# A gated linear scan with a soft mixture of experts on one core: slot sums divided behind the experts, some gates by sigmoid, PSUM banks held in pairs, and a new order table

## The chip, the cores and the metric

The kernel runs on one core of one Trainium2 chip. The metric is the device time of one execution in microseconds (us). The core has five instruction streams that work side by side: PE (the matrix engine; "PEld" is its weight load), DVE (vector), ACT (scalar, table functions), POOL (a second vector engine) and SP, which here only issues DMAs. SBUF holds tiles of 128 partitions; PSUM has 8 banks of 128 x 512 float32, which PE writes and DVE and ACT read.

## The reference, cut to what matters

```python
# x, r_gate, i_gate: (4, 5056, 256); 20224 tokens of 256 channels
log_a = 8.0 * sigmoid(r_gate) * log(sigmoid(a_param))      # per token and channel
a_t = exp(log_a)
x_gated = sqrt(max(1 - a_t * a_t, 1e-6)) * sigmoid(i_gate) * x
h = a_t[:, t] * h + x_gated[:, t]                           # along the 5056 tokens of a batch: y
logits = y @ phi                                            # 32 slots, 8 experts of 4
d = exp(logits - logits.max(0));  d /= d.sum(0) + 1e-9      # over all 20224 tokens
slot_input = d.T @ y                                        # (32, 256)
slot_out[e] = relu(slot_input[e] @ w1[e]) @ w2[e]           # w1 (8,256,1024), w2 (8,1024,256)
c = exp(logits - logits.max(1));  c /= c.sum(1) + 1e-9
out = c @ slot_out
```

## The kernel before, in words

Line numbers of before stand first, those after the change behind a slash.

**Windows.** The tokens are cut into 40 windows of 512 (the last has 256), and the windows into units of one or two. For each window three DMAs bring r, i and x. PE transposes r into PSUM (`rp`, L383/L394), so that channels lie on partitions and time lies along a row, and ACT reads each half of that from its bank into `A` (`sr`, L393/L406: tanh of r/2). Per unit ACT takes the sigmoid of i (`si`, L405/L427), POOL multiplies i by x (`u`, L412/L434), ACT forms a_t (`ex`, L425/L448 and L450, an Exp whose scale and bias are read from a 128 x 1 column), POOL squares it (`sq`, L433/L458) and ACT takes the square root of 1 - a² (`qr`, L440/L465). PE transposes u into PSUM (`up`, L450/L475); DVE multiplies it there, in place, by the root (`st`, L460/L485) and scans along time (`sc`, L473/L498), reading the bank. PE transposes the scanned rows back (`yp`, L493/L518), and DVE or ACT copies them out of PSUM (`yc`, L281 and L279/L288 and L286). Every such step is named by window and half: `sc 22 1` is the scan of window 22, half 1.

**Groups.** Four windows make a group: logits (`lp`, L539/L573), their running maximum on DVE (`ls`, L549 and L552/L583 and L586), the factor for the older groups on ACT (`md`, L557/L591), transposes of the logits (`ep`, L563/L597), their Exp on ACT (`ee`, L572/L606), the weighted sums on PE (`acc`, L581/L615) and their accumulation on DVE (`as`, L592/L626).

**Slots and experts.** Behind the last group some small steps form the weights of the groups (`Wt`). In before `sp` (L656 and L657) sums the groups with them, tokens' sums and denominators both, and `slot` (L662 to L664) takes the reciprocal of the denominators and multiplies. The experts run in four pairs (`hp` L713/L755, `hs`, `ht`, `hr`, `so` L740/L782), then `s0`, `s1` and `s2` spread their result.

**Tokens.** For each group the weights c over the slots are formed (`ct`, `c0`, `cm`, `c1` L802/L847, `c2`, `c3`, `hc`, `hx`), PE multiplies (`op`, L839/L884: 16 matmuls into four banks), DVE and ACT copy the four banks out (`og`, L281 and L279/L288 and L286) and a DMA of 512 KB stores each window.

**What sets the order.** Every step is an operation with a number; the string `ORDER` lists the numbers, `b` behind one puts it on its second engine. `Plan.order` walks the list with costs written in the code, starts an operation when its engine, its inputs and its buffers are free, and so chooses the buffers; the instructions are then emitted in that order, each engine takes its own in that order, and the framework puts in the waits between engines, which keep the accesses to each tile in the order of the program. ACT holds one table of functions at a time; the list groups the square roots of three or four units, then the sigmoids, then the exponentials, with a table load at each change.

Of the kernel before, what the change touches and what calls it, by code (L numbers as in the profile page):

```python
# [8 lines left out]
F32 = mybir.dt.float32  # L9
# [8 lines left out]
N_ES = 2  # L18
TABLE_US = 1.283
# [22 lines left out]
394 434 454 475 495 862 417 395 320 863 360 864 865 361 866 396 418 397 338 297 340 398 399 339b 435 321 322b  # L42
341b 298b 414 415 379 868 380b 476 400 416 381 362 299 363 419 300 489 629 507 529 651 508 432 632 382 453 472
436 439 875 613 633 614 513 473 876 656 437 440 877 634 455 458 869 878 515 867 635 597 657 438 441 480 459 481
456 879 460 457 494 514 870 871 872 873 477 401 420 654 442 556 880 516 536 874 478 482 402 421 403 422 423b 655
496 499 404 443 497 500 444 461 445 479 462 498 517 598 618 557 577 881 518 882 521 463 883 884 886 501 522 519
464 523 502 503 520 589 711 530 733 611 549 671 571 548 570 885 535 483 714 485 887 504 540 524 630 590 612 652
752 693 774 599 558 554 555 595 576 617 888 541 526 486b 715 738 739 675 736 525b 636 737 527 542 505 537 538
757 559 755 697 673 756 758 484 539 674 676 677 562 560 563 543 578 716 717 889 698 561 579 564 544 581 779 695
890 777 696 780 778 891 580 638 720 679 582 631 653 793 672 694 596 603 604 637 658 622 619 600 641 892 893 894  # L50
895 620 583 601 623 605 602 678 897 898 624 639 659 721 741 680 700 640 899 621 584 585 586 565 587b 566b 567
660 642 896 625 626b 568b 545 643 546 661 606 722 607b 681 663 627 644 628 645 662 646 608 796 901 682 685 713
815 963 754 753 975 712 776 794 795 734 983 775 816 817 735 699 902 900 761 609b 718 908 701 686 664 683 665 702
# [33 lines left out]
class Plan:  # L87
# [42 lines left out]
    def order(self):  # L130
        out = []
# [775 lines left out]
```

## Time and profile before

| | us |
|---|---|
| median of 3 runs | 307.64 (307.35 to 307.68) |
| the profiled execution | 307.92 |
| its span, first to last instruction | 306.1 |
| PE, DVE, ACT, POOL busy | 241.1, 238.0, 246.1, 181.7 |
| mean granted TensorE clock | 0.928 |

The profile is of one execution. A row "L393 ACT ACTIVATE g<-b ... x78 | 41.5, 609 | 2.5 <-PE b L383" reads: line 393, on ACT, from a bank (b) into a buffer (g), 78 instructions, 41.5 us in all, 609 ns the mean of one, and 2.5 us in which ACT stood idle ahead of them, mostly until the PE instruction of line 383 had ended. A row of the stretches lists for each engine the busy time inside the stretch and the number of instructions, then the granted clock of PE (1.00 is full speed), the mean busy share of the DMA engines and their GB/s.

### The profile page before, as it was taken

What the parts mean: (1) busy time and instruction counts of PE and PEld (TensorE: products, weight loads), DVE (VectorE), ACT (ScalarE), POOL (GpSimd) and SP (SyncE); (2) the same over time, 40 slices, a digit from 0 to 9 for tenths busy, and PEclk for the clock granted to TensorE, in tenths of its full rate; (3) what the DMA queues carried; (4) which work ended last, traced back from release to release, by engine and by line L of the source; (5) the groups of instructions that cost most, each with busy time, mean ns of one, the idle gap of its engine ahead of it and who ended that gap; (6) DMA issues with size and microseconds to landing.
All of it is one profiled execution on the core that took longest, in us unless ns stands there. A gap on an engine that the chain in (4) does not pass through costs nothing.

```text
span 306.1 us, 5779 instructions
## 1 busy us (share of the span) xinstructions
PE 241.1 (79%) x2134; PEld 170.0 (56%) x2134; DVE 238.0 (78%) x370; ACT 246.1 (80%) x311; POOL 181.7 (59%) x121
## 2 busy tenths in 40 slices
PE   3605797969888896988989788878999999898900
PEld 3604665737646754766577464736563677656700
DVE  0003999699999998999999989979967869975600
ACT  5999999999999999999999999997220457874320
POOL 1389986988598899699599996991000241031000
PEclk9955999999999999799999999999999999995565
DMA  7999999967998993998856997999990019999996
GB/s 252 415 405 408 408 376 412 396 255 286 399 383 323 410 365 122 378 413 281 327 207 238 384 363 305 335 385 349 406 359 6 2 60 401 405 403 407 361 409 269
DMA packets 28032, 100.03 MB, mean 327 GB/s; under 512 B 3362, under 2 KB 3364, under 8 KB 28004
## 3 DMA queue, kind: packets, MB, share of 16 engines
q1 hardware_dynamic: 28004, 99.66, 84.8%
q8 instruction: 17, 0.28, 0.4%
q14 instruction: 11, 0.09, 0.1%
HBM read 78.94 MB, written 20.71 MB: 326 GB/s over the span
## 4 chain that ended last, share of the span: by engine, by line
PE 25%; ACT 25%; DVE 15%; issue 9%; POOL 6%; DMA 3%; ACTq 0%; SPq 0%; DVEq 0%; POOLq 0%
PE b L839 7%; ACT g L425 7%; DVE g L473 6%; ACT g L393 5%; DVE b L460 4%; ACT g L405 4%; POOL g L412 3%; ACT g L440 3%; POOL g L433 2%; DVE y L281 2%; PE b L713 2%; PE b L740 2%; PE b L493 2%; PE b L450 2%; ACT y L279 2%
## 5 line engine op out<-in xcount | busy, mean ns | idle before, releaser
L412 POOL TENSOR_TENSOR g<-g,g 128x1024 f32<-128x1024 f32 (+1 forms) x40 | 92.7, 2347 | 10.6 <-ACT g L405 10.1
L433 POOL TENSOR_TENSOR g<-g 128x1024 f32<-128x1024 f32 (+1 forms) x40 | 73.8, 1873 | 25.0 <-ACT g L425 21.9
L460 DVE SCALAR_TENSOR_TENSOR b<-g,b 128x512 f32<-128x512 f32 (+1 forms) x80 | 51.5, 677 | 31.4 <-ACT g L440 30.2
L450 PE MATMUL b<-ident,g 128*128 128x128 f32 x316 | 47.6, 286 | 21.7 <-POOL g L412 15.5
L493 PE MATMUL b<-ident,g 128*128 128x128 f32 x316 | 46.9, 283 | 10.4 <-DVE g L473 4.1
L450 PEld LDWEIGHTS b<-ident,g 128*128 128x128 f32 x316 | 35.8, 145 | 34.1 <-POOL g L412 17.7
L383 PE MATMUL b<-ident,g 128*128 128x128 f32 x316 | 46.5, 288 | 8.1 <-DMA g<-in_r_gate_dram 3.2
L473 DVE TENSOR_TENSOR_SCAN g<-g,g,b 128x512 f32<-128x512 f32 x40 | 50.3, 1271 | 0.2
L473 DVE TENSOR_TENSOR_SCAN g<-g,b 128x512 f32<-128x512 f32 (+7 forms) x46 | 49.2, 1094 | 0.3
L493 PEld LDWEIGHTS b<-ident,g 128*128 128x128 f32 x316 | 35.1, 143 | 23.7 <-DVE g L473 8.6
L425 ACT ACTIVATE g<-g,ca 128x1024 f32<-128x1024 f32 (+2 forms) x44 | 47.5, 1158 | 0.0
L810 POOL TENSOR_TENSOR y<-y,rs 128x512 f32<-128x512 f32 x10 | 10.4, 1048 | 61.3 <-DVE rs L807 59.8
L383 PEld LDWEIGHTS b<-ident,g 128*128 128x128 f32 x316 | 36.4, 146 | 18.0 <-ACT g L393 4.3
L393 ACT ACTIVATE g<-b 128x512 f32<-128x512 f32 x80 | 42.2, 605 | 2.5 <-PE b L383 2.4
L281 DVE COPY y<-b 128x512 f32<-128x512 f32 x55 | 36.4, 678 | 6.9 <-PE b L814 3.5
L405 ACT ACTIVATE g<-g 128x2048 f32<-128x2048 f32 (+2 forms) x22 | 38.2, 1755 | 0.1
L440 ACT ACTIVATE g<-g 128x2048 f32<-128x2048 f32 (+2 forms) x22 | 37.2, 1736 | 0.1
L279 ACT COPY g<-b 128x512 f32<-128x512 f32 x47 | 24.7, 593 | 14.3 <-PE b L839 13.5
L839 PE MATMUL b<-soR,y 32*128 32x256 f32 x320 | 31.2, 462 | 3.4 <-DVE y L281 2.3
L839 PEld LDWEIGHTS b<-soR,y 32*128 32x128 f32 x320 | 22.0, 219 | 10.0 <-ACT g L279 3.2
L281 DVE COPY g<-b 128x512 f32<-128x512 f32 x33 | 21.0, 680 | 5.1 <-PE b L839 4.8
L279 ACT COPY y<-b 128x512 f32<-128x512 f32 x34 | 18.7, 592 | 5.9 <-PE b L493 5.9
(83 smaller groups left out, 244.0 us busy)
## 6 DMA issues: line engine op xcount, KB each, us to landing
g<-in_x_dram SPq DMA_DIRECT2D x39, 512.0 KB, 6.7
g<-in_i_gate_dram SPq DMA_DIRECT2D x39, 512.0 KB, 8.1
out_dram<-g SPq DMA_DIRECT2D x39, 512.0 KB, 6.2
g<-in_r_gate_dram SPq DMA_DIRECT2D x38, 512.0 KB, 6.6
g<-in_moe_w_dram SPq DMA_DIRECT2D x32, 512.0 KB, 6.3
g<-in_r_gate_dram SPq DMA_DIRECT2D x3, 256.0 KB, 5.8
g<-in_i_gate_dram SPq DMA_DIRECT2D x1, 256.0 KB, 8.9
g<-in_x_dram SPq DMA_DIRECT2D x1, 256.0 KB, 8.8
```

Source lines behind the costliest of these rows:

```text
L281: nc.vector.tensor_copy(out=dst, in_=srct)
L383: nc.tensor.transpose(out=by_tile(rp, n)[:, j, :], in_=rows(("r", w), n)[:, j, h * P : (h + 1) * P], identity=ident,)
L393: nc.scalar.activation(halves(("A", w))[:, h, :c], Bk(("rp", w, h))[:, :c], AF.Tanh, scale=0.5)
L405: nc.scalar.activation(a, a, AF.Sigmoid)
L412: nc.gpsimd.tensor_tensor(out=rows(("x", w), n), in0=rows(("i", w), n), in1=rows(("x", w), n), op=ALU.mult)
L425: nc.scalar.activation(a, a, AF.Exp, scale=ca[:, h : h + 1], bias=ca[:, h : h + 1])
L433: nc.gpsimd.tensor_tensor(out=halves(("N", w))[:, :, :c], in0=a, in1=a, op=ALU.mult)
L450: nc.tensor.transpose(out=by_tile(up, n)[:, j, :], in_=rows(("x", w), n)[:, j, h * P : (h + 1) * P], identity=ident,)
L460: nc.vector.scalar_tensor_tensor(up, halves(("N", w))[:, h, :c], 1e-3, up, op0=ALU.max, op1=ALU.mult)
L473: nc.vector.tensor_tensor_scan(dst, dst, up[:, s0:s1], init, op0=ALU.mult, op1=ALU.add)
L493: nc.tensor.transpose(out=yp[:, j, h * P : (h + 1) * P], in_=halves(("A", w))[:, h, (2 * i + j) * P : (2 * i + j + 1) * P], identity=ident,)
L839: nc.tensor.matmul(Bk(("op", w0, n))[:, i * D : (i + 1) * D], hT()[r, (2 * i2 + i) * P : (2 * i2 + i + 1) * P], soR[r, :], start=True, sto ...
```

## The change

- The third pair of `sp` matmuls, which summed the denominators, and the two DVE steps that divided are gone; `slot` is one copy. In their place `dn` (four small matmuls, L698) and `rd` (an addition and a reciprocal on 128 x 1, L703 and L704) run later, and `s2`, behind the experts, multiplies by `rd`.
- Where all `sr` of a unit are emitted while the sigmoid table is loaded, `sr` takes Sigmoid instead of tanh, and `ex` reads only a scale column (`ca8`, eight times the logarithm) and no bias column. This holds for 6 units: 12 of the 44 `ex` instructions (L448).
- The 8 PSUM tiles of one bank (`bank`) become 4 tiles of two banks (`banks`, 128 x 2 x 512), and `Bk` returns a half of one. Variants that would use both halves at once are written but are switched off (`WIDE_R`, `WIDE_Y`).
- The planner's costs are written anew, `acc` also depends on the first `yc` of each window, and `ORDER` is a new list of 1237 operations (1235 before). There are 24 table loads in both. ACT does 25 of the `yc` copies instead of 29.

```diff
+WIDE_R = False
+WIDE_Y = False
...
 ORDER = """
-1 74 96 5 33 11 115 55 13 12 34 56 75 116 4 35 219 137 57 241 97 159 301 76 138 160 98 179 201 117 2 0 6 7 8 9
+1 74 96 5 115 2 0 3 6 7 8 9 10 77 79 101 99 118 78 102 80 100 119 120 83 121 11 16 14 15 33 55 36 58 124 17 60
...
-    bank = [ps.tile([P, C], F32, name=f"b{i}") for i in range(8)]
+    banks = [ps.tile([P, 2, C], F32, name=f"b{i}") for i in range(4)]
...
     def Bk(key):
-        return bank[plan.place[key]]
+        i = plan.place[key]
+        return banks[i // 2][:, i % 2, :]
...
     def e_decay3(o):
+        nc.vector.tensor_scalar(ca8, ca, 8.0, None, op0=ALU.mult)
         nc.vector.tensor_scalar(ca, ca, 4.0, None, op0=ALU.mult)
...
+    def plain(unit):
+        return all(plan.by_key[("sr", v, h)].table == "S" for v in unit for h in range(1 if WIDE_R else H))
...
-                nc.scalar.activation(halves(("A", w))[:, h, :c], Bk(("rp", w, h))[:, :c], AF.Tanh, scale=0.5)
+
+                f, k = (AF.Sigmoid, 1.0) if plain(unit) else (AF.Tanh, 0.5)
+                nc.scalar.activation(halves(("A", w))[:, h, :c], Bk(("rp", w, h))[:, :c], f, scale=k)
...
-                    nc.scalar.activation(a, a, AF.Exp, scale=ca[:, h : h + 1], bias=ca[:, h : h + 1])
+                    if plain(unit):
+                        nc.scalar.activation(a, a, AF.Exp, scale=ca8[:, h : h + 1])
+                    else:
+                        nc.scalar.activation(a, a, AF.Exp, scale=ca[:, h : h + 1], bias=ca[:, h : h + 1])
...
-               deps=[("ee", t), ("acc", t, j - 1)] + [("yc", w, j // 2) for w in ws],
+               deps=[("ee", t), ("acc", t, j - 1)] + [("yc", w, i) for w in ws for i in {0, j // 2}],
...
     def e_sp(o):
         for h in range(H):
             nc.tensor.matmul(sp()[:, h, :], accS[:, h * P : (h + 1) * P], Wt, start=True, stop=True)
-        nc.tensor.matmul(
-            sp()[:, H, :], accS[:, D : D + 1].broadcast_to([P, P]), Wt, start=True, stop=True
-        )
...
     def e_slot(o):
-        nc.vector.tensor_scalar(rd, sp()[:, H : H + 1, :], 1e-9, None, op0=ALU.add)
+        nc.vector.tensor_copy(out=slotT, in_=sp())
+
+
+    def e_dn(o):
+        for j in range(J):
+            nc.tensor.matmul(
+                Bk(("dn",))[32 * j : 32 * j + NS, :1], Wt, accS[:, D : D + 1], start=True, stop=True
+            )
+
+    def e_rd(o):
+        nc.vector.tensor_scalar(rd, Bk(("dn",))[:, :1], 1e-9, None, op0=ALU.add)
         nc.vector.reciprocal(rd, rd)
-        nc.vector.tensor_tensor(out=slotT, in0=sp()[:, :H, :], in1=rd.broadcast_to([P, H, NS]), op=ALU.mult)
...
     def e_s2(o):
-        copy(o, soR, Bk(("sr",))[:, :D])
+        if o.on == "ACT":
+            nc.scalar.activation(soR, Bk(("sr",))[:, :D], AF.Copy, scale=rd)
+        else:
+            nc.vector.tensor_scalar(soR, Bk(("sr",))[:, :D], rd, None, op0=ALU.mult)
```

The rows below stand as the built programs have them: line, operation, target<-source with the number of each tile, shape, and the engines (and DMA rings) whose semaphores the instruction waits on. A tile b is PSUM: in before b0_88 to b7_95 are one bank each, after the change b0_88 to b3_91 are two banks each, and the two halves bear one name.

**ACT behind the roots of windows 6 to 11.** In before ACT ends the sigmoids of this phase with these rows; the last four are `sr 20 1`, `sr 18 0`, the table load and the first exponential of windows 12 and 13:

```order
L393 ACTIVATE g6_67<-b2_90 128x512 [waits PE_49]
L393 ACTIVATE g6_67<-b1_89 128x512 [waits DVE_49,PE_49]
L393 ACTIVATE g13_74<-b3_91 128x512 [waits PE_49,Pool_49]
L405 ACTIVATE g1_62<-g1_62 128x2048 [waits DMAHW2_49,DMAHW1_49,Activation_49]
L393 ACTIVATE g13_74<-b6_94 128x512 [waits DVE_49,PE_49]
L393 ACTIVATE g2_63<-b4_92 128x512
L425 ACT_TABLE_LOAD
L425 ACTIVATE g16_77<-g16_77,ca_108 128x2x512
```

After the change ACT has there the last sigmoids of this phase, with `sr 14 1` and `sr 27 0` (the third and fourth row), the exponential of windows 12 and 13, and behind it `sr 16 0`, which reads a half of b3 and waits for DVE:

```order
L406 ACTIVATE g18_79<-b0_88 128x512 [waits PE_49]
L427 ACTIVATE g10_71<-g10_71 128x2048 [waits DMAHW5_49,DMAHW2_49]
L406 ACTIVATE g1_62<-b1_89 128x512 [waits PE_49]
L406 ACTIVATE g18_79<-b2_90 128x512
L450 ACT_TABLE_LOAD
L450 ACTIVATE g3_64<-g3_64,ca_104 128x2x512 [waits Activation_49]
L450 ACTIVATE g3_64<-g3_64,ca_104 128x2x512
L406 ACTIVATE g16_77<-b3_91 128x512 [waits DVE_49,PE_49]
L406 ACTIVATE g16_77<-b0_88 128x512 [waits PE_49]
```

What moved: eleven `sr` instead of eight stand between the roots and this table load, and the semaphore that `sr 16 0` waits on at DVE stands for `yc 7 1`, the copy out of the other half of b3.

**DVE at windows 7 to 10.** In before the two multiplications of window 9 (the third and fourth row) come behind `ls 1`, and a copy and the scans of the same window follow:

```order
L549 TENSOR_SCALAR l1_97,m1_121<-b0_88,m0_120 128x512 [waits PE_49]
L552 SCALAR_TENSOR_TENSOR n1_132<-b0_88,m1_121,minus_110 128x1 [waits DVE_49]
L460 SCALAR_TENSOR_TENSOR b5_93<-g10_71,b5_93 128x512 [waits DMAHW3_49,Pool_49]
L460 SCALAR_TENSOR_TENSOR b1_89<-g10_71,b1_89 128x512 [waits PE_49,Activation_49]
L281 COPY y1_81<-b7_95 128x2x256
L473 SCALAR_TENSOR_TENSOR g0_61<-g0_61,b5_93 128x448 [waits DVE_49]
L473 SCALAR_TENSOR_TENSOR g0_61<-g0_61,b5_93 128x64
L473 SCALAR_TENSOR_TENSOR g0_61<-g0_61,b1_89 128x448 [waits DVE_49]
```

After the change window 9, half 1 (`st 9 1`, the fourth row) comes first of windows 8 and 9, straight behind the last scan of window 7:

```order
L485 SCALAR_TENSOR_TENSOR b2_90<-g18_79,b2_90 128x512 [waits DVE_49]
L288 COPY y0_80<-b1_89 128x2x256 [waits PE_49]
L498 SCALAR_TENSOR_TENSOR g16_77<-g16_77,b2_90 128x512 [waits PE_49,Activation_49]
L485 SCALAR_TENSOR_TENSOR b2_90<-g8_69,b2_90 128x512 [waits PE_49,DMAHW7_49,Activation_49,Pool_49]
L485 SCALAR_TENSOR_TENSOR b3_91<-g8_69,b3_91 128x512
L485 SCALAR_TENSOR_TENSOR b3_91<-g8_69,b3_91 128x512 [waits DVE_49]
L498 SCALAR_TENSOR_TENSOR g11_72<-g11_72,g16_77,b3_91 128x512 [waits DVE_49]
```

What moved: `st 9 1` works in a half of b2, and the ACT semaphore that it waits on stands for `sr 27 0`, which reads the other half of b2 (the fourth row of the ACT piece above). Behind it on DVE stand windows 8 to 10 and, sixteen rows on, `yc 7 1`.

**ACT and DVE behind the roots of windows 18 to 23.** In before ACT had, from the last of these roots on:

```order
L440 ACTIVATE g12_73<-g12_73 128x2048 [waits Pool_49]
L405 ACT_TABLE_LOAD [waits DMAHW4_49]
L405 ACTIVATE g7_68<-g7_68 128x2048 [waits DMAHW2_49]
L393 ACTIVATE g15_76<-b3_91 128x512 [waits DMAHW6_49,DVE_49,PE_49]
L393 ACTIVATE g0_61<-b4_92 128x512 [waits DVE_49,PE_49]
L405 ACTIVATE g1_62<-g1_62 128x2048 [waits DMAHW5_49,DMAHW4_49]
L572 ACT_TABLE_LOAD
L572 ACTIVATE e0_86<-b0_88 128x512 [waits Activation_49]
```

After the change it has, from the first copy behind these roots on, `ee 3` and `sr 31 0` as the last two rows:

```order
L286 COPY y3_83<-b2_90 128x2x256 [waits DVE_49]
L427 ACT_TABLE_LOAD [waits DMAHW7_49]
L427 ACTIVATE g12_73<-g12_73 128x2048 [waits DMAHW4_49]
L406 ACTIVATE g13_74<-b0_88 128x512 [waits PE_49,Activation_49]
L406 ACTIVATE g13_74<-b0_88 128x512
L406 ACTIVATE g15_76<-b1_89 128x512 [waits DVE_49,PE_49]
L427 ACTIVATE g2_63<-g2_63 128x2048 [waits DMAHW1_49,DMAHW0_49]
L406 ACTIVATE g11_72<-b3_91 128x512 [waits DVE_49,PE_49,Pool_49]
L591 ACT_TABLE_LOAD
L591 ACTIVATE d3_142<-m2_119,n3_131 128x1
L606 ACTIVATE e0_86<-b1_89 128x512 [waits DVE_49,PE_49]
L406 ACTIVATE g13_74<-b2_90 128x512 [waits DVE_49,PE_49]
```

And on DVE, after the change, the end of window 21, the first half of window 22, `ls 4` (its two rows in the middle) and `sc 22 1` behind it:

```order
L498 SCALAR_TENSOR_TENSOR g4_65<-g4_65,b3_91 128x512 [waits DVE_49]
L485 SCALAR_TENSOR_TENSOR b0_88<-g1_62,b0_88 128x512 [waits DVE_49,Pool_49]
L485 SCALAR_TENSOR_TENSOR b2_90<-g1_62,b2_90 128x512 [waits PE_49]
L498 SCALAR_TENSOR_TENSOR g7_68<-g7_68,g4_65,b0_88 128x512 [waits DVE_49]
L583 TENSOR_SCALAR l4_96,m4_121<-b1_89,m3_120 128x512
L586 SCALAR_TENSOR_TENSOR n4_132<-b1_89,m4_121,minus_107 128x1 [waits DVE_49]
L498 SCALAR_TENSOR_TENSOR g7_68<-g7_68,g4_65,b2_90 128x512
```

What moved: `ee 3` of before waited on DVE for nothing; after the change it waits for `ls 4`, which reads the logits of the next group in the other half of b1, and `sr 31 0` waits for `sc 22 1`, which reads the other half of b2.

Over the program the instructions of the four engines wait on each other at 1264 places in before. In 1254 the awaited instruction touched the same buffer region, and in 4 only another part of the same tile. After the change 319 of such waits are on an instruction that touched only the other half of a two-bank tile: ACT on PE 34, ACT on DVE 45, DVE on ACT 39, DVE on PE 53, DVE on itself 37, PE on ACT 45, PE on DVE 66.

More of the change, by code (lines that the diff above doesn't have):

```diff
@@ L155, in order @@
                 table = o.act[0]
-            o.start, o.end = t, t + us
+            o.start, o.end, o.table = t, t + us, table
             free[e] = o.end
@@ L228, in Bk, with Bk2 @@
     def Bk(key):
-        return bank[plan.place[key]]
+        i = plan.place[key]
+        return banks[i // 2][:, i % 2, :]
+    def Bk2(key):
+        return banks[plan.place[key] // 2]
     def rows(key, n):
@@ L256 @@
     ca = const.tile([P, H], F32, name="ca")
+    ca8 = const.tile([P, H], F32, name="ca8")
     ones = const.tile([1, 1], F32, name="ones")
@@ L266 @@
     wj = const.tile([P, 1], F32, name="wj")
-    rd = const.tile([P, 1, NS], F32, name="rd")
+    rd = const.tile([P, 1], F32, name="rd")
     mrun = [const.tile([P, 1], F32, name=f"m{g}") for g in range(NGR + 1)]
@@ L376, in window @@
         for o_, nm in enumerate("rix"):
-            op(("L" + nm, w), "DMA", (2.6 if (nm, w) == ("i", 0) else 1.29) * f, load(nm), alloc=gets(nm), uses=has(nm))
+            op(("L" + nm, w), "DMA", 1.29 * f, load(nm), alloc=gets(nm), uses=has(nm))
         def e_rp(h):
@@ L391, in emit, with e_srw @@
             def emit(o):
-                nc.scalar.activation(halves(("A", w))[:, h, :c], Bk(("rp", w, h))[:, :c], AF.Tanh, scale=0.5)
-            return emit
+                f, k = (AF.Sigmoid, 1.0) if plain(unit) else (AF.Tanh, 0.5)
+                nc.scalar.activation(halves(("A", w))[:, h, :c], Bk(("rp", w, h))[:, :c], f, scale=k)
+            return emit
+        def e_srw(o):
+            f, k = (AF.Sigmoid, 1.0) if plain(unit) else (AF.Tanh, 0.5)
+            nc.scalar.activation(halves(("A", w))[:, :, :c], Bk2(("rp", w, 0))[:, :, :c], f, scale=k)
         for h in range(H):
             op(("rp", w, h), "PE", 0.5 * f, e_rp(h), deps=[("Lr", w), ("ident",)],
-               alloc=[("B", ("rp", w, h))], uses=[("r", w)])
-            op(("sr", w, h), "ACT", 0.05 + 0.43 * f, e_sr(h), deps=[("rp", w, h)],
-               alloc=gets("A") if h == 0 else [], uses=[("rp", w, h)] + ([("A", w)] if h or not first else []),
-               act="ES")
+               alloc=[("B2", ("rp", w, 0), ("rp", w, 1))] if WIDE_R and h == 0 else [] if WIDE_R else [("B", ("rp", w, h))],
+               uses=[("r", w)] + ([("rp", w, 1)] if WIDE_R and h else []))
+            if not WIDE_R:
+                op(("sr", w, h), "ACT", 0.05 + 0.43 * f, e_sr(h), deps=[("rp", w, h)],
+                   alloc=gets("A") if h == 0 else [], uses=[("rp", w, h)] + ([("A", w)] if h or not first else []),
+                   act="ES")
+        if WIDE_R:
+            op(("sr", w, 0), "ACT", 0.07 + 0.85 * f, e_srw, deps=[("rp", w, 0), ("rp", w, 1)],
+               alloc=gets("A"), uses=[("rp", w, 0), ("rp", w, 1)] + has("A"), act="ES")
         def e_si(o):
```

108 lines of the change are left out of this document (59 added, 49 removed), and 30 rows, old and new, of the table ORDER.

## The prediction

> **What bounds the kernel now.** I read first the stretches of the span, cut where the chain of waits changes engine, and then the groups of instructions by line. The stretches, with the columns us, PE, PEld, DVE, ACT, POOL busy, granted clock, DMA share and GB/s:
>
> ```profile
> 27.64:205.44 177.80, 150.97 (x1294) 107.92 (x1292) 168.19 (x229) 177.24 (x194) 154.79 (x93) 0.98 0.89 338
> 205.44:219.65 14.21, 12.80 (x112) 8.49 (x112) 13.96 (x20) 8.55 (x15) 2.13 (x1) 1.00 1.00 373
> 219.65:229.36 9.71, 9.70 (x87) 6.21 (x84) 7.16 (x22) 2.86 (x8) 0.00 (x0) 1.00 0.95 380
> 229.36:246.30 16.94, 16.94 (x210) 8.51 (x209) 12.39 (x31) 3.78 (x7) 3.39 (x4) 1.00 0.01 4
> 250.50:306.10 55.60, 36.67 (x348) 26.72 (x341) 32.59 (x60) 28.43 (x55) 5.20 (x5) 0.76 0.96 374
> ```
>
> For 178 us ACT is the bound: 177.24 of 177.80 us busy, up to the last root. DVE has 9.6 us of room there, PE 27. Then DVE is full for 14 us (the last scans), PE for 10 and for the 17 of the experts, and the last 56 us are the stores' (DMA share 0.96). So whatever makes ACT stand still between 27.6 and 205.4 us lengthens the run one for one, and DVE can lose 9.6 us before it does the same. The groups that carry the sums (instructions, busy us, mean ns, idle time before them and its releaser), and last a row of the waits (us in total, times, longest):
>
> ```profile
> L393 ACT ACTIVATE g<-b 128x512 f32<-128x512 f32 x78 | 41.5, 609 | 2.5 <-PE b L383 2.4
> L405 ACT ACTIVATE g<-g 128x2048 f32<-128x2048 f32 x18 | 34.7, 1931 | 0.1
> L440 ACT ACTIVATE g<-g 128x2048 f32<-128x2048 f32 x18 | 33.7, 1912 | 0.1
> L405 ACT ACT_TABLE_LOAD x7 | 9.0, 1283 | 0.1
> L425 ACT ACTIVATE g<-g,ca 128x1024 f32<-128x1024 f32 x36 | 42.2, 1243 | 0.0
> L572 ACT ACTIVATE e<-b 128x512 f32<-128x512 f32 x9 | 5.4, 598 | 0.1
> L557 ACT ACTIVATE d<-m,n 128x1 f32<-128x1 f32 x8 | 2.3, 285 | 0.0
> L279 ACT COPY y<-b 128x512 f32<-128x512 f32 x34 | 18.7, 592 | 5.9 <-PE b L493 5.9
> L460 DVE SCALAR_TENSOR_TENSOR b<-g,b 128x512 f32<-128x512 f32 x78 | 50.8, 684 | 31.4 <-ACT g L440 30.2 <-PE b L450 0.7 <-ACT e L572 0.3
> L473 DVE TENSOR_TENSOR_SCAN g<-g,g,b 128x512 f32<-128x512 f32 x40 | 50.3, 1271 | 0.2
> L281 DVE COPY y<-b 128x512 f32<-128x512 f32 x55 | 36.4, 678 | 6.9 <-PE b L814 3.5 <-ACT g L279 1.9 <-PE b L493 1.5
> L549 DVE TENSOR_SCALAR_CACHE_REDUCE l<-b,m 128x512 f32<-128x512 f32 x8 | 5.9, 738 | 0.0
> L552 DVE SCALAR_TENSOR_TENSOR n<-b,m,minus 128x1 f32<-128x1 f32 x9 | 2.0, 219 | 0.4
> ...
> DVE b L460 <- ACT g L440: 30.2, 5, 23.9
> ```
>
> The idle columns say why it runs so well: the 78 `sr` lost only 2.5 us, all for PE; ACT's other rows lost next to nothing, none of it for DVE. DVE's own 31.4 us are for the roots, 23.9 of them in one wait, the first. Neither engine waits on the other except through the roots.
>
> **The change part by part.** First what it saves.
>
> ```profile
> L425 ACT ACTIVATE g<-g,ca 128x512 f32<-128x512 f32 x6 | 4.7, 834 | 0.0
> L802 ACT ACTIVATE y<-y 128x512 f32<-128x512 f32 x10 | 5.9, 629 | 1.0 <-DVE y L799 1.0
> 225.14 0.24 PE L638 MATMUL b<-ones,mmax 1*32 1x1 f32 x8
> 227.55 0.63 PE L656 MATMUL b<-Wt,accS 128*128 128x32 f32 x4
> 228.01 0.39 PE L657 MATMUL b<-Wt,accS 128*128 128x32 f32 x2
> 228.44 0.19 DVE L662 TENSOR_SCALAR rd<-b 128x32 f32<-128x32 f32 x1 [0.95 <-PE b L657]
> 229.05 0.22 DVE L664 TENSOR_TENSOR slotT<-b,rd 128x64 f32<-128x64 f32 x1
> ```
>
> *Gates.* An Exp with two columns as operands takes 834 ns, one of the same shape with none 629: 0.10 us a column. Twelve `ex` lose one: 12 x 0.10 = 1.2 us of ACT (bounds 0 and 2.5, both columns). Sigmoid in place of tanh I take at nothing, as the table stays loaded; the 609 ns of L393 and 598 of L572, both of one shape, bound it at 0.01 us each. *Copies.* Two of the four `yc` that leave ACT stand before its last root: 2 x 0.59 = 1.2 us; DVE takes 4 x 0.68 = 2.7, inside its 9.6 us of room. *Slots.* The `sp` pairs end 228.01 + 0.39 - (227.55 + 0.63) = 0.22 us earlier, and between 228.44 and 229.05 DVE's 0.61 us go; `dn` comes back as four small matmuls on a full PE (at most the 0.24 us of L638), `rd` lies beside the experts, and the column in `s2` costs 0.10: 0.5 us saved (bounds 0.8 and a loss of 0.2). Together 2.9 us.
>
> *Pairs of banks.* Here I put the weight. The counts and the rows of the section on the change show that 319 waits now are on an instruction that touched only the other half of a two-bank tile, 45 of them ACT on DVE and 39 DVE on ACT. They cost nothing if the awaited instruction is done; so I laid both engines' order between two groups of roots side by side, each instruction at its mean from the rows above, time zero at the end of the group's first root, when DVE may begin.
>
> Roots 6 to roots 12. ACT does 2 `qr`, a table, 3 `si` and 11 `sr`, the last `sr 27 0`: 3.82 + 1.28 + 5.79 + 6.70 = 17.6 us. DVE reaches `st 9 1` far earlier (4 `st`, 4 `sc`, 2 `yc` and a short row: under 10 us) and, as this waits for `sr 27 0`, stands still for about 8 us. From there to `yc 7 1` it has 6 `st`, 5 `sc`, 2 `yc`, 1 `ls` (0.96 us with its second row): 4.10 + 6.36 + 1.36 + 0.96 = 12.8, so `yc 7 1` ends at 30.4. `sr 16 0`, which waits for it, is due on ACT at 17.6 + 1.28 + 2 x 1.24 = 21.4. ACT stalls 9.0 us.
>
> Roots 18 to roots 24. `ee 3` is due on ACT after 2 `qr`, a `yc`, 2 tables, 2 `si`, 4 `sr` and `md`: 3.82 + 0.59 + 2.57 + 3.86 + 2.44 + 0.29 = 13.6 us. It waits for `ls 4`, before which DVE has 10 `st`, 9 `sc`, 2 `yc`: 6.84 + 11.44 + 1.36 + 0.96 = 20.6. Stall 7.0; then `sr 31 0` waits for `sc 22 1` (20.6 + 1.27 = 21.9, due at 21.2): 0.7 more, 7.7 in all.
>
> Roots 12 to roots 18. `sr 19 0`, due at 8.3 (2 `qr`, table, `si`, 2 `sr`), waits for `sc 14 0` (5 `st`, 5 `sc`, 1 `yc`: 10.5): 2.2. Then DVE's `st 15 1` waits for `sr 19 1` until 15.4 and `ls 2` for `sr 24 0` until 18.0; from there `ls`, 3 `st`, 3 `sc`, 3 `yc` (8.9) to `sc 15 1` at 26.8, for which `sr 28 0`, due at 20.8 + 2.2 = 23.0, waits: 3.9 more, 6.1 in all.
>
> The other three stretches have waits of the same two kinds (`sr 7 0` on `sc 4 0`, `sr 32 0` on `ls 5`, `st 34 0` on a copy of window 31), and I give them the mean, 7.6: six times 7.6 is 46 us. Of what is left out, hand-overs lengthen this and overlap of neighbouring instructions shortens it:
>
> ```profile
> 205.32 1.06 ACT L279 COPY y<-b 128x512 f32<-128x512 f32 x2
> ```
>
> Two copies of 0.59 take 1.06 us, a tenth less than their sum. Bounds: 23 us if DVE's room and later slack give half back, and 54 if all six stall like the worst.
>
> *Behind the roots.* Nothing of the last scans, slots and experts gains, and a few waits of the same kind stand there (`slot` on a transpose for the token weights); I take 2 us, bounds 0 and 4. The stores:
>
> ```profile
> 250.09 1.32 PE L839 MATMUL b<-soR,y 32*128 32x256 f32 x16
> 280.00:285.00 5.00, 3.81 (x25) 2.65 (x25) 2.58 (x4) 3.06 (x6) 0.00 (x0) 0.50 1.03 410
> 283.88:290.85 6.97, 6.96 (x64) 5.37 (x64) 4.27 (x8) 2.53 (x5) 0.00 (x0) 0.61 1.00 352
> ```
>
> A window's `op` takes 1.32 us at full clock and 6.97 / 4 = 1.74 where 0.61 was granted. Its four banks are now two tiles, whose halves must be copied one after the other (0.59 + 0.68); with hand-overs of 0.2 to 0.4, a set of tiles turns round in 2.9 us at full clock and 3.4 at the lower, and two sets alternate: 1.45 to 1.7 us a window against the 55.6 / 39.5 = 1.41 that the stores take. Over 39 windows that is 2 to 11 us; I take 4, as the larger part ran at a clock over 0.6.
>
> The sum goes against the profiled execution's 307.9 us (span 306.1 and 1.8 around it, 0.3 above the median of 307.64): 307.9 - 2.9 = 305.0 without the pair waits, and 305.0 + 46 + 2 + 4 = **357 us**.
>
> **The rivals.** *The waits are always over (305.0, faster).* If DVE ran so far ahead that every awaited half was long done, only the 2.9 us of savings would remain. It decides if DVE needs under 13.6 us to `ls 4`; its rows say 20.6, and the room of 9.6 us in 178 speaks against such a lead. The Trainium skill ("PSUM — Partial Sum Buffer", on bank collisions) asks for guarding by bank and quadrant, so by its rule no wait between the halves would be needed and the time would be this 305.0; no run here shows two engines in two banks of a pair at once. It says what the program could leave out, the program has the waits. Chance 0.04.
>
> *Half is given back (331).* Each stall of ACT lets loads, POOL and PE run ahead, and the two engines fall into step: 305 + 23 + 3 = 331. For it: DVE's 9.6 us and the 52 of the 80 `sr` that wait for no instruction of DVE. Against: in the two worked stretches DVE was itself held first. Chance 0.2.
>
> *PE falls to the low clock in the stalls (375).*
>
> ```profile
> 20.00:25.00 5.00, 0.00 (x0) 0.00 (x0) 0.00 (x0) 4.97 (x5) 4.97 (x3) 0.50 1.03 410
> 25.00:30.00 5.00, 3.73 (x16) 3.14 (x16) 2.33 (x3) 4.97 (x5) 5.00 (x4) 0.51 1.04 413
> ```
>
> An idle PE was granted 0.50, and 0.51 for the next 5 us though it was 3.73 busy. Spread over 224 us (178 + 46), PE's 151 us in the first stage are 67% busy instead of 85. If a third of its work ran at 0.5, it would grow by 50 us, to 201 of 224, and every transpose on the way of a wait would take 0.57 instead of 0.29; I put that at 3 us for each of six stretches: 357 + 18 = 375. The Trainium skill ("TensorE: Matmul & The Clock Gate", Part 1) halves the clock only after an idle window of about 3.4 us; the stretch from 280 us differs, where 0.50 was granted with PE 3.81 of 5 us busy. By the page only the stalls over 3.4 us would count, and the low clock would last about as long behind each; an estimate from that is 6 x 1.7 = 10 us. Chance 0.13.
>
> **How the numbers follow.** 357 has 0.6 (own range 343 to 370), half given back 0.2 (324 to 343), low clock 0.13 (370 to 388), waits always over 0.04; 0.03 is left for sizes outside these. The range, 326 to 384, leaves out the first rival and the outer ends of the other two. Under 0.2% a measurement of this kernel can't tell from no change. Faster 0.04, same 0.02, slower 0.94.
>
> **What would show it.** Right: ACT busy share under 0.9 up to the last root, an idle column at L406 and L606 released by DVE (L498, L583, L288) of 30 us or more, an idle column at L485 released by ACT b L406, and the last root at 245 to 255 us instead of 205. The gates' part: L448 0.1 us shorter than L450 at the same shape. The slots: under 0.3 us from the last `sp` to `slot`. Wrong: L406 with an idle column of a few us as L393 has now, or stalls that PE, not DVE, releases.

## The result and the profile after

The changed kernel takes 463.95 us (median of 4 runs, 463.75 to 466.57), before 307.5 us (4 runs, 306.7 to 307.68): a ratio of 1.511 (1.506 to 1.518). The forecast was slower, at 357 us and at most 384. The side was right; the size was a third of what came, +49 us where +156 were measured.

Here is where the time went. Both spans are cut at the same four places: the end of the last root (a half-size one; the prediction's 205.4 is the end of the last full one), the first matmul of the experts, the first store, the end. The stretches of before (us, PE, PEld, DVE, ACT, POOL busy, granted clock, DMA share, GB/s):

```profile
0.00:207.84 207.84, 162.55 (x1362) 118.16 (x1363) 171.23 (x239) 202.80 (x227) 171.31 (x111) 0.96 0.90 342
207.84:229.36 21.52, 20.78 (x184) 13.29 (x183) 18.76 (x36) 9.01 (x20) 0.00 (x0) 1.00 0.97 373
229.36:250.55 21.19, 21.19 (x250) 11.87 (x253) 15.45 (x38) 5.91 (x12) 5.21 (x5) 1.00 0.01 3
250.55:306.10 55.55, 36.62 (x348) 26.67 (x341) 32.54 (x60) 28.38 (x55) 5.20 (x5) 0.76 0.96 374
```

and those of the changed kernel:

```profile
0.00:329.91 329.91, 201.87 (x1373) 150.40 (x1373) 181.01 (x245) 205.71 (x228) 171.59 (x111) 0.80 0.59 221
329.91:355.20 25.29, 20.56 (x170) 13.76 (x170) 16.74 (x32) 6.75 (x14) 0.00 (x0) 0.93 0.68 248
355.20:381.53 26.33, 20.36 (x244) 10.53 (x245) 15.85 (x40) 5.23 (x10) 4.56 (x5) 1.00 0.01 2
381.53:462.30 80.77, 49.56 (x356) 31.68 (x354) 35.71 (x62) 28.49 (x53) 5.78 (x6) 0.62 0.66 257
```

The four stretches grew by 122.1, 3.8, 5.1 and 25.2 us. In the first, ACT has nearly the same work (202.8 and 205.7 us busy) but was busy for 98% of the stretch before and for 62% after. Nothing has taken its place: PE is at 61%, DVE at 55%, POOL at 52%, the DMA engines at 59%. The bound is no engine any more; it is the waits between them. The groups say who waits for whom (busy us, mean ns, idle time before them and its three main releasers):

```profile
L485 DVE SCALAR_TENSOR_TENSOR b<-g,b 128x512 f32<-128x512 f32 x78 | 52.1, 688 | 90.0 <-PE b L394 34.5 <-ACT g L406 17.4 <-PE b L475 8.7
L406 ACT ACTIVATE g<-b 128x512 f32<-128x512 f32 x78 | 43.3, 601 | 78.8 <-PE b L394 32.6 <-DVE g L498 13.7 <-DVE y L288 9.6
L606 ACT ACTIVATE e<-b 128x512 f32<-128x512 f32 x9 | 5.4, 597 | 19.0 <-PE b L475 9.8 <-DVE n L586 8.6 <-PE b L600 0.6
L394 PE MATMUL b<-ident,g 128*128 128x128 f32 x316 | 57.8, 333 | 36.7 <-DVE g L498 26.7 <-ACT g L406 7.4 <-DMA g<-in_r_gate_dram 2.4
L518 PE MATMUL b<-ident,g 128*128 128x128 f32 x316 | 56.3, 320 | 30.1 <-ACT g L406 9.8 <-DVE g L498 9.1 <-ACT y L286 5.7
```

The idle time before `sr` (L406) went from 2.5 us to 78.8. Some releasers have no data to give: `sr` reads the transposes of r, and neither a scan (L498) nor a copy to y (L288) makes those; `yp` (L518) needs scanned rows, not `sr`. What stands there is the other half of the tile. `rp` (L394) waits 26.7 us for scans: before, 0.7. The prediction worked out three stretches between roots. The ACT stalls of two of them stand in the trace, at `sr 16 0`, and at `ee 3` with `sr 31 0` behind it; the row between them here is `sr 19 0`, of the third (start, us, instruction, idle time before it):

```profile
122.37 1.09 ACT L406 ACTIVATE g<-b 128x512 f32<-128x512 f32 x2 [9.64 <-DVE y L288]
147.48 1.09 ACT L406 ACTIVATE g<-b 128x512 f32<-128x512 f32 x2 [1.96 <-PE b L394]
208.60 0.60 ACT L606 ACTIVATE e<-b 128x512 f32<-128x512 f32 x1 [8.56 <-DVE n L586]
209.78 0.60 ACT L406 ACTIVATE g<-b 128x512 f32<-128x512 f32 x1 [0.59 <-DVE g L498]
```

9.64 us were forecast as 9.0, 8.56 and 0.59 as 7.0 and 0.7. In the third stretch `sr 19 0` was to wait 2.2 us for DVE and `sr 28 0` 3.9; the first waits 1.96, but for PE, and the second does not wait at all. So the long stalls that I walked are there at about their size, and there are many more that I did not walk. A piece of 14 us between the roots of windows 12 and 18, all engines in one view, shows of what kind:

```profile
149.41 1.93 ACT L427 ACTIVATE g<-g 128x2048 f32<-128x2048 f32 x1
151.21 0.62 ACT L406 ACTIVATE g<-b 128x512 f32<-128x512 f32 x1
151.68 1.94 ACT L427 ACTIVATE g<-g 128x2048 f32<-128x2048 f32 x1
...
151.97 1.09 PE L475 MATMUL b<-ident,g 128*128 128x128 f32 x4 [2.66 <-ACT g L406]
...
152.85 1.06 PE L394 MATMUL b<-ident,g 128*128 128x128 f32 x4
...
153.70 1.06 PE L518 MATMUL b<-ident,g 128*128 128x128 f32 x4
...
154.56 0.76 PE L475 MATMUL b<-ident,g 128*128 128x128 f32 x4
...
155.42 0.69 DVE L288 COPY y<-b 128x512 f32<-128x512 f32 x1 [8.69 <-PE b L475]
...
158.29 1.97 PE L475 MATMUL b<-ident,g 128*128 128x128 f32 x8 [2.97 <-DVE b L485]
...
160.05 1.06 PE L518 MATMUL b<-ident,g 128*128 128x128 f32 x4
...
160.90 0.99 PE L394 MATMUL b<-ident,g 128*128 128x128 f32 x4
...
161.94 0.60 ACT L406 ACTIVATE g<-b 128x512 f32<-128x512 f32 x1 [7.39 <-PE b L394]
```

ACT runs a sigmoid of i before its `sr`; PE's `up` (L475) waits for that `sr`, which read the other half; three more groups of transposes stand behind it in PE's queue; DVE waits 8.69 us for the last of them; PE then waits for DVE; ACT waits 7.39 us for the `rp` behind that. ACT and DVE wait for PE, and PE was waiting for the two of them.

### The profile page after: what moved, and what is told of

The parts are those of the page before. It is cut to its first block, busy times and chain, and to the rows that moved or that the text cites. A ratio compares the mean times of both kernels' runs of the same rounds, so it can differ in the third digit from the quotient of the medians.

```text
span 462.3 us, 5765 instructions
## 1 busy us (share of the span) xinstructions
PE 292.3 (63%) x2140; PEld 206.4 (45%) x2140; DVE 249.3 (54%) x378; ACT 246.2 (53%) x304; POOL 181.9 (39%) x121
## 5 line engine op out<-in xcount | busy, mean ns | idle before, releaser
L434 POOL TENSOR_TENSOR g<-g,g 128x1024 f32<-128x1024 f32 (+1 forms) x38 | 87.8, 2328 | 54.4 <-ACT g L427 39.8
L458 POOL TENSOR_TENSOR g<-g 128x1024 f32<-128x1024 f32 (+1 forms) x40 | 74.3, 1872 | 75.0 <-issue 20.1
L485 DVE SCALAR_TENSOR_TENSOR b<-g,b 128x512 f32<-128x512 f32 (+1 forms) x80 | 52.9, 681 | 90.0 <-PE b L394 34.5
L406 ACT ACTIVATE g<-b 128x512 f32<-128x512 f32 (+1 forms) x80 | 44.1, 597 | 78.8 <-PE b L394 32.6
L475 PE MATMUL b<-ident,g 128*128 128x128 f32 x316 | 58.6, 327 | 38.1 <-POOL g L434 12.7
L394 PE MATMUL b<-ident,g 128*128 128x128 f32 x316 | 57.8, 333 | 36.7 <-DVE g L498 26.7
L518 PE MATMUL b<-ident,g 128*128 128x128 f32 x316 | 56.3, 320 | 30.1 <-ACT g L406 9.8
L475 PEld LDWEIGHTS b<-ident,g 128*128 128x128 f32 x316 | 44.6, 170 | 52.0 <-issue 21.1
L394 PEld LDWEIGHTS b<-ident,g 128*128 128x128 f32 x316 | 46.5, 174 | 47.7 <-DVE g L498 26.8
L518 PEld LDWEIGHTS b<-ident,g 128*128 128x128 f32 x316 | 43.3, 165 | 45.3 <-DVE g L498 12.2
L288 DVE COPY y<-b 128x512 f32<-128x512 f32 x60 | 40.3, 683 | 42.2 <-PE b L518 22.1
L498 DVE TENSOR_TENSOR_SCAN g<-g,g,b 128x512 f32<-128x512 f32 x40 | 50.4, 1271 | 10.3 <-PE b L394 4.1
L498 DVE TENSOR_TENSOR_SCAN g<-g,b 128x512 f32<-128x512 f32 (+7 forms) x46 | 49.4, 1095 | 8.0 <-PE b L475 4.2
L884 PE MATMUL b<-soR,y 32*128 32x256 f32 x320 | 40.9, 579 | 17.8 <-DVE y L844 7.0
L855 POOL TENSOR_TENSOR y<-y,rs 128x512 f32<-128x512 f32 x10 | 10.3, 1047 | 96.4 <-DVE rs L852 85.4
L286 ACT COPY g<-b 128x512 f32<-128x512 f32 x46 | 24.9, 595 | 40.2 <-PE b L884 25.2
L884 PEld LDWEIGHTS b<-soR,y 32*128 32x128 f32 x320 | 24.9, 271 | 30.1 <-ACT g L286 16.6
L615 PE MATMUL b<-y,e 128*32 128x257 f32 x316 | 26.3, 447 | 13.6 <-ACT g L406 7.6
L286 ACT COPY y<-b 128x512 f32<-128x512 f32 x29 | 16.6, 588 | 33.6 <-PE b L518 13.9
L288 DVE COPY g<-b 128x512 f32<-128x512 f32 x34 | 22.1, 685 | 22.6 <-PE b L884 16.5
```

What stands on the lines that cost most here:

```text
L286: nc.scalar.copy(out=dst, in_=srct)
L288: nc.vector.tensor_copy(out=dst, in_=srct)
L394: nc.tensor.transpose(out=by_tile(rp, n)[:, j, :], in_=rows(("r", w), n)[:, j, h * P : (h + 1) * P], identity=ident,)
L406: nc.scalar.activation(halves(("A", w))[:, h, :c], Bk(("rp", w, h))[:, :c], f, scale=k)
L434: nc.gpsimd.tensor_tensor(out=rows(("x", w), n), in0=rows(("i", w), n), in1=rows(("x", w), n), op=ALU.mult)
L458: nc.gpsimd.tensor_tensor(out=halves(("N", w))[:, :, :c], in0=a, in1=a, op=ALU.mult)
```

## The experiments

Twelve kernels were run. Where no interval is given it was one run beside before at 307.6 to 308.3 us; the runs of before on one chip lie up to 1.1% apart, so one per cent in a single run says nothing.

**Which part of the change it is.** The first pair undoes the pairing alone, and does it alone.

```diff
-    banks = [ps.tile([P, 2, C], F32, name=f"b{i}") for i in range(4)]
+    bank = [ps.tile([P, C], F32, name=f"b{i}") for i in range(8)]
...
-        i = plan.place[key]
-        return banks[i // 2][:, i % 2, :]
+        return bank[plan.place[key]]
```

> The changed kernel with eight tiles of one bank instead of four of two; nothing else differs, the order of every engine stays. Only 2 waits on another part of a tile are left of 319. Theory A (the pair waits carry the whole loss): 303 to 307 us, the 2.9 us of savings of the prediction at best. Theory B (the new order or the new operations are to blame, the waits only show it): over 400 us.

Measured: 304.58 us (303.55 to 305.18) where before took 308.33 on the same chip, a ratio of 0.988 (0.984 to 0.991). With the same order of work on every engine the whole loss (theory A's claim) is gone and a gain of 1.2% stands. ACT's `sr` waits as little as in before (L405 is the same instruction here):

```profile
L405 ACT ACTIVATE g<-b 128x512 f32<-128x512 f32 x78 | 42.4, 604 | 2.8 <-PE b L393 2.5
```

The reverse edit in the kernel before:

```diff
-    bank = [ps.tile([P, C], F32, name=f"b{i}") for i in range(8)]
+    banks = [ps.tile([P, 2, C], F32, name=f"b{i}") for i in range(4)]
```

> The kernel before with four tiles of two banks instead of eight of one; its order, gates and slot sums stay. It has 353 waits on the other half of a tile. Theory A: 430 to 490 us, as far up as the change went. Theory B: 306 to 312 us.

Measured: 487.45 us. The old order suffers yet more (353 such waits against 319). Theory B has fallen: neither the new order nor the new operations cost anything.

**How the cost grows.** Two pairs are kept, four banks stand alone:

```diff
+    banks = [ps.tile([P, 2, C], F32, name=f"b{i}") for i in range(2)]
+    bank = [ps.tile([P, C], F32, name=f"s{i}") for i in range(4)]
...
+        return banks[i // 2][:, i % 2, :] if i < 4 else bank[i - 4]
```

> The changed kernel with two of the four pairs split into tiles of one bank; 182 waits on the other half are left of 319. Theory A with a cost in proportion to the waits: 305 + 157 x 182 / 319 = 395 us (370 to 420). A cost that comes only when all buffers are coupled: under 340. Theory B: over 440.

Measured: 395.04 us, the figure of the proportion: 182 of the 319 waits cost 90 of the 159 us (463.95 against 304.6), about half a microsecond each on average.

**Is it PE's own work?** In the paired kernel each group of four transposes issues the first alone (the banks are filled with zeros once at the start):

```diff
-                for j in range(n):
+                for j in range(1):
                     nc.tensor.transpose(
                         out=by_tile(rp, n)[:, j, :],
```

and so for the gated x and for the scanned rows.

> The changed kernel with the pairs, in which each group of four transposes of r, of the gated x and of the scanned rows issues only its first; three quarters of those three are left out, so the output is not the reference's. PE loses about 130 of its 292 us of work, the waits between the halves stay (298). Theory A1 (the loss is the other engines' work strung one behind the other by the waits, PE only passes them on): 410 to 450 us. Theory A2 (PE's own work, at a clock that falls in the stalls, is what stands in the chain): under 360 us.

Measured: 431.71 us. With three quarters of the transposes gone 32 of the 159 us went; 127 stayed, counted from the one-bank kernel with all its transposes, as none with so few was run. Theory A2 has fallen: the time of these transposes, the lower clock with it, is the lesser part.

**Which waits.** In the next four the tiles are of one bank, as in the first, and the waits are put back by hand for chosen pairs of engines:

```diff
+    coupled = {("ACT", "DVE"), ("DVE", "ACT")}
...
+            for i in halves_used:
+                for eng, name in last[i ^ 1].items():
+                    if (o.on, eng) in coupled:
+                        tc.add_manual_dep(new[0], name, sync, reason="pair")
+            for i in halves_used:
+                last[i][o.on] = new[-1].name
```

Here `last` holds for each bank the last instruction of each engine on it, and `i ^ 1` is the other bank of the pair. The control with all six pairs of engines:

> One-bank tiles with all these explicit waits (about 280): the waits of the paired tiles without the pairing. All theories in which the waits are the cause: 440 to 480 us, near the 464 of the change. If the place or shape of the tiles had a part of its own: under 400.

Measured: 463.68 us, where the change took 463.95. So the waits are all of the loss; the place and shape of the tiles have no part in it that these runs could show. Nor have the 37 waits of DVE on itself, which were not put back. ACT and DVE alone:

> The changed kernel with one-bank tiles (304.6 us), and explicit waits put back only between ACT and DVE: whoever uses one bank of a pair waits for the last use of the other bank by the other of the two (83 waits). Theory P (the prediction's walk priced these waits rightly; the rest of the loss, about 110 us, is PE's waits, which it left out): 335 to 365 us. Theory Q (the walk was too short for ACT and DVE themselves): over 400. Theory R (these waits cost little unless PE is coupled too): under 320.

Measured: 376.61 us, 72 above the 304.6 without. It lies between the limits of theories P and Q: the walk was short, but this is less than half the loss. The stalls of the walk stand in its trace too, at `st 9 1` (forecast about 8), at `sr 16 0` (9.0) and at `ee 3` (7.0), and smaller than walked at `sr 19 0` (2.2) and `sr 28 0` (3.9), the third and fourth row:

```profile
90.23 1.89 DVE L484 SCALAR_TENSOR_TENSOR b<-g,b 128x512 f32<-128x512 f32 x3 [6.76 <-ACT g L405]
104.05 1.09 ACT L405 ACTIVATE g<-b 128x512 f32<-128x512 f32 x2 [10.22 <-DVE y L287]
126.11 2.07 ACT L405 ACTIVATE g<-b 128x512 f32<-128x512 f32 x4 [1.28 <-DVE g L497]
141.14 1.09 ACT L405 ACTIVATE g<-b 128x512 f32<-128x512 f32 x2 [1.39 <-DVE g L497]
175.04 0.60 ACT L605 ACTIVATE e<-b 128x512 f32<-128x512 f32 x1 [7.72 <-DVE n L585]
```

All waits with PE at one end, none between ACT and DVE:

> One-bank tiles with explicit waits only where PE is one of the two: PE on ACT and DVE, ACT and DVE on PE (about 210 waits), none between ACT and DVE. Theory P: 380 to 430 us, more than the ACT and DVE waits cost. Theory Q: under 350. Theory R: over 430, nearly the whole.

Measured: 433.23 us, 129 above; 3 us over the upper limit of theory P and just inside that of R. Then the two directions apart, PE waiting, and PE waited for:

> One-bank tiles with explicit waits only of PE: PE waits for the last use of the other bank of the pair by ACT and by DVE (about 115 waits); ACT and DVE wait for nothing new. If PE's queue, in which one waiting transpose holds up all behind it, is what spreads the loss: 350 to 400 us. If it is the mutual waiting, back and forth, that costs: 310 to 335.

Measured: 388.37 us, 84 above. And:

> One-bank tiles with explicit waits only of ACT and of DVE on PE's last use of the other bank of the pair (about 95); PE waits for nothing new. If PE's own queue is the spreader: under 345 us, well below the 388 with the waits of PE alone. If each direction costs alike: 370 to 400.

Measured: 335.2 us, 31 above. About 115 waits of PE cost 84 us, about 95 on PE 31. Both together cost 129, more than their sum of 115. The waits between ACT and DVE (72 alone) add only 30 to that, as all together cost 159: these two kinds partly cover each other. In the first of the two kernels ACT has no new wait, yet loses as much before `sr` as when it is coupled to DVE, because PE arrives late. First the row of the kernel with ACT and DVE coupled:

```profile
L405 ACT ACTIVATE g<-b 128x512 f32<-128x512 f32 x78 | 42.9, 604 | 42.5 <-DVE g L497 17.0 <-PE b L393 12.0 <-DVE y L287 10.2
```

then that of the kernel in which PE alone waits:

```profile
L405 ACT ACTIVATE g<-b 128x512 f32<-128x512 f32 x78 | 43.4, 595 | 43.1 <-PE b L393 34.3 <-PE b L572 5.1 <-issue 3.4
```

and that of the kernel in which PE has no new wait, where ACT loses less than half:

```profile
L405 ACT ACTIVATE g<-b 128x512 f32<-128x512 f32 x78 | 42.7, 606 | 18.5 <-PE b L393 6.2 <-POOL g L433 5.2 <-PE b L572 3.4
```

So of the waits with PE, those that stand in PE's own queue cost the most: about 0.7 us each, against 0.3 for a wait on PE (a wait between ACT and DVE cost 0.9 with none of the others there).

The table sets these kernels side by side by the time from one group of roots to the next (from table load to table load), each against the one-bank kernel, and by the time behind the last load:

| waits put back | 0-6 | 6-12 | 12-18 | 18-24 | 24-30 | 30-36 | sum | behind |
|---|---|---|---|---|---|---|---|---|
| none (length itself) | 31.9 | 30.2 | 29.9 | 26.5 | 30.1 | 27.6 | 176.1 | 101.6 |
| ACT with DVE | +14.4 | +10.3 | +8.6 | +12.1 | +7.2 | +5.9 | +58.5 | +13.7 |
| PE on them | +17.3 | +4.6 | +13.9 | +10.6 | +10.6 | +8.5 | +65.5 | +18.1 |
| them on PE | +1.2 | +8.8 | +0.7 | +3.6 | +3.5 | +2.1 | +19.9 | +10.2 |
| all with PE | +18.7 | +16.9 | +20.2 | +11.4 | +13.2 | +13.6 | +94.0 | +34.2 |
| all, by hand | +21.6 | +18.1 | +19.5 | +16.9 | +13.6 | +20.1 | +109.8 | +48.8 |
| the change | +22.5 | +19.9 | +19.9 | +18.3 | +13.7 | +18.6 | +112.9 | +46.3 |

**What the rest of the change is worth.** With one-bank tiles, the gates' part, the slots' part and both were taken back:

```diff
     def plain(unit):
-        return all(plan.by_key[("sr", v, h)].table == "S" for v in unit for h in range(1 if WIDE_R else H))
+        return False
```

> The changed kernel with one-bank tiles and without the gates' part: every unit takes tanh and the Exp with scale and bias columns again. If the twelve lost columns are worth the 1.2 us of the prediction: a ratio to before about 0.004 higher than the 0.988 with the gates (305.5 to 306.5 us on a chip where before takes 307.6). If the gates give nothing: the same ratio.

Measured: 305.2 us, a ratio of 0.992 (0.990 to 0.994).

```diff
     def e_slot(o):
-        nc.vector.tensor_copy(out=slotT, in_=sp())
+        nc.vector.tensor_scalar(rd, sp()[:, H : H + 1, :], 1e-9, None, op0=ALU.add)
+        nc.vector.reciprocal(rd, rd)
+        nc.vector.tensor_tensor(out=slotT, in0=sp()[:, :H, :], in1=rd.broadcast_to([P, H, NS]), op=ALU.mult)
```

with the third pair of `sp` matmuls back, `dn` and `rd` gone, and `s2` a plain copy.

> The changed kernel with one-bank tiles and with the slot sums divided ahead of the experts, as in before (its third pair of matmuls, its three DVE steps; no dn and rd). If the slots are worth the prediction's 0.5 us: a ratio 0.002 above 0.988, hardly to be told from it. If the whole 1.5 us between the last sums and the experts were won: 0.005 above.

Measured: 304.22 us, 0.990 (0.988 to 0.992).

> The changed kernel with one-bank tiles and with neither the gates' part nor the slots' part: what is left is the new order table and its moved copies. If gates, slots and copies make the gain as the prediction priced them: a ratio of 0.994 to 0.997. If the order alone makes it: 0.988.

Measured: 305.62 us, 0.993 (0.992 to 0.995). The order alone gains 0.7% (0.5 to 0.8), 2.1 us. With the gates it is 0.990 and without 0.993, a difference of about 1 us whose intervals overlap a little. With the slots 0.992 against 0.993: not resolved. The gates are seen in the rows of the changed kernel, without and with the bias column:

```profile
L448 ACT ACTIVATE g<-g,ca 128x1024 f32<-128x1024 f32 x12 | 12.9, 1142 | 0.0
L450 ACT ACTIVATE g<-g,ca 128x1024 f32<-128x1024 f32 x24 | 28.3, 1245 | 0.0
```

## Why the prediction was wrong

**What held.** *The cause and the side:* the waits on the other half make all of the loss, 319 of them by tile (463.95) or about 280 by hand (463.68) against 304.6 without. *The kernel without them:* 305.0 forecast; 0.988 x 307.6 = 303.8 measured (302.7 to 304.9). The gates were priced at 0.10 us an instruction and cost 1245 - 1142 = 103 ns; the order gave 2.1 us where the copies were priced at 1.2; the slots' 0.5 us lie below what the runs resolve. *The longest stalls that were walked* (in the changed kernel, and with the waits of ACT and DVE alone): `sr 16 0` 9.0 forecast, 9.6 and 10.2 measured; `ee 3` 7.0, measured 8.6 and 7.7.

**The step that failed: the walk took two queues, and left PE's out of all six stretches.** The prediction named 319 waits, 198 of them with PE at one end, and then "laid both engines' order between two groups of roots side by side", ACT's and DVE's. PE was taken as a hand-over. Its rows invited that: 27 us of room, and 286 ns for a transpose. But room is no cover for a queue in order. A transpose that waits for ACT holds back the next one, which DVE needs, and so on round. The term of 46 us for the first stage measured 58.5 with the waits of ACT and DVE alone, which is a fair walk of the queues it walked: 9.0, 6.1 and 7.7 stood for 10.3, 8.6 and 12.1, and the mean of 7.6 for 14.4, 7.2 and 5.9 in the stretches not worked. Part of that is luck: in the stretch of the 8.6 the two stalls that were walked make only 1.28 + 1.39 us. With all waits the term measured 112.9. The missing part of about 54 us in the first stage came with PE's waits: all with PE at one end make 94.0 there by themselves, PE's own 65.5. The counts in the prediction pointed there, 198 of 319; walking three queues instead of two would have been the step to take.

**Behind the last table load: 6 us forecast, 46 measured** (44 against before). About 10 of them come before the last root has ended, which is 15.5 us behind that load, against 5.6 in before. Most of that is one copy on ACT, which waits for a multiply in the other half of its tile:

```profile
324.66 0.59 ACT L286 COPY y<-b 128x512 f32<-128x512 f32 x1 [7.02 <-DVE b L485]
```

Between the last root and the experts' start, and up to the first store, 8.9 us were lost where 2 were taken. The stores' 4 us became 25.2, and there the working itself was wrong in two places. It took an `op` of 16 matmuls for one window's; there are 20 of them (320 matmuls on L839), so one serves two. This error alone made the forecast too high: 20 turns of 1.45 to 1.7 us, 29 to 34 us in all, would hide behind 55.6 us of stores. The other error made it too low: it let two sets of whole tiles alternate. In the program only 5 of the 20 have their four banks in two whole tiles; the other 15 hold one whole tile and two halves whose other halves belong to someone else, the next `op` among them. So two neighbours seldom overlap. The trace shows some of them one behind the other, each held by a copy out of PSUM:

```profile
440.06 2.09 PE L884 MATMUL b<-soR,y 32*128 32x256 f32 x16 [1.36 <-DVE g L288]
442.88 2.12 PE L884 MATMUL b<-soR,y 32*128 32x256 f32 x16 [0.73 <-ACT g L286]
445.71 3.36 PE L884 MATMUL b<-soR,y 32*128 32x256 f32 x16 [0.71 <-ACT g L286]
```

Over the last stretch an `op` took 80.77 / 20 = 4.0 us against 55.55 / 20 = 2.8 in before, and DMA share fell from 0.96 to 0.66: the stores are no longer the bound. How much of the 25.2 us is the lower clock (0.62 against 0.76 in before) stays open.

**The rivals.** *The waits are always over:* its price was right (303.8), as the one-bank tiles show, which take these waits away; its condition, that the waits are over in time, did not hold in the changed kernel. The Trainium skill's rule in "PSUM — Partial Sum Buffer", on bank collisions, to guard by bank and quadrant, is borne out as far as that: eight tiles guarded one by one do the same work with none of these waits. *Half is given back* went the wrong way; stalls made more stalls. *PE at the low clock:* the clock fell, from 0.96 to 0.80 in the first stretch, and a transpose from 286 to 320 to 333 ns. But a kernel with a quarter of the transposes lost 127 of the 159 us all the same. The third group of transposes of the changed kernel:

```profile
L475 PE MATMUL b<-ident,g 128*128 128x128 f32 x316 | 58.6, 327 | 38.1 <-POOL g L434 12.7 <-DVE y L288 8.6 <-DVE g L498 6.1
```

The three hold 57.8 + 56.3 + 58.6 = 172.7 us, against 141.0 before. If the 32 us between them weigh like the transposes that were left out (32 us of time for about 130 of work), the clock is worth some 8 us for these three; this is an estimate from these rows, and no run held the clock apart.

**The signs named beforehand.** ACT's share under 0.9: 0.62. Idle time at L406 and L606 released by DVE of 30 us or more: 40.5, of which 13.7 + 9.6 at L406 and 8.6 at L606 stand in the rows above, and 8.6, for `sr 32 0`, in a row of the waits:

```profile
ACT g L406 <- DVE n L586: 8.6, 1, 8.6
```

Idle time at L485 released by ACT's `sr`: 17.4. The last root at 245 to 255 us: 330. And the sign against, "stalls that PE, not DVE, releases": the largest releaser at L406 is PE with 32.6. That was the warning of what was left out. The slots' sign failed in the changed kernel too:

```profile
353.77 0.57 PE L690 MATMUL b<-Wt,accS 128*128 128x32 f32 x4
354.18 0.70 PE L835 MATMUL b<-ident,l 128*128 128x128 f32 x4
354.92 0.22 DVE L693 COPY slotT<-b 128x64 f32<-128x64 f32 x1 [1.26 <-PE b L835]
```

The copy should follow less than 0.3 us behind `sp`; it stands 0.58 us behind it, as it waits for the transposes of `ct` (L835) in the other half. With one-bank tiles it follows at once:

```profile
225.19 0.53 PE L689 MATMUL b<-Wt,accS 128*128 128x32 f32 x4
...
225.75 0.22 DVE L692 COPY slotT<-b 128x64 f32<-128x64 f32 x1 [0.89 <-PE b L689]
```


**What stays open.** How the loss of a wait splits between clock and order was only estimated. As the kinds of waits cover and lengthen each other, what each of them costs depends on which others are there. The one-bank kernel, at 0.988 of before, has the lowest ratio of the versions that were run; with the slots' part taken back it is at 0.990 (0.988 to 0.992), which these runs can't tell from it.

## What to carry to other kernels

How large a tile is declared decides what waits for what, even if no instruction touches more: two banks under one name made 319 waits and 159 us, on average half a microsecond a wait, without one more operation. When an edit adds waits, walk every queue that has one, the engine with room as well: an engine that takes its instructions in order passes a wait on to all that stands behind it, and waits in both directions cost more than the two directions apart (129 us with PE, 84 and 31 apart). And count how often an operation runs, and which buffers it has, before pricing it: 320 matmuls by 16 would have said 20, and their places in PSUM that only 5 of the 20 have two whole tiles.

## What the runs showed of the hardware beyond that

The clock of PE stays low, and also falls, where PE pauses only briefly. A stretch of the changed kernel among the stores:

```profile
435.00:450.00 15.00, 10.49 (x68) 5.92 (x67) 6.77 (x11) 4.16 (x8) 0.00 (x0) 0.50 0.62 226
```

PE was busy for 10.49 of 15 us and was granted 0.50; the rows of L884 above lie in it, with gaps of 0.71 to 1.36 us, and 16 matmuls take 2.09 us there against 1.32 in before at full clock. The Trainium skill ("TensorE: Matmul & The Clock Gate", Part 1) has the half clock follow an idle window of about 3.4 us, and the full clock a busy one of about that length. The stay at 0.50 agrees with the second: no piece of work in these rows is longer than 3.36 us. With the first the trace does not agree. Three stretches of the changed kernel between the roots, cut where the clock changes:

```profile
134.39:137.81 3.42, 1.40 (x14) 1.16 (x12) 2.73 (x5) 3.40 (x3) 3.42 (x2) 1.00 0.25 84
137.81:141.22 3.41, 3.41 (x17) 1.45 (x16) 3.13 (x5) 2.15 (x2) 1.62 (x2) 0.50 0.17 70
141.22:148.05 6.83, 4.35 (x36) 2.91 (x34) 5.48 (x7) 1.76 (x4) 3.51 (x2) 1.00 0.65 230
```

In the first PE was busy for 1.40 of 3.42 us, and its longest pause was 2.02 us; still the clock fell to 0.50 behind it, for 3.41 us in which PE was busy throughout, and then came back.
